# PSUM as three fixed groups of neighbouring banks, VectorE products over two banks at once, and a new order of the opening, in a fused sketch-attention and MLP kernel

## The chip, the cores and the metric

The kernel runs on one core of a Trainium2 chip. The metric is device time in microseconds (us), the median of several executions. A single execution can fall in a slower state (over 1.5% above the fastest run of the same kernel on the chip); such runs are listed but not compared. The engines are TensorE (PE in the profile, its weight loads PEld), VectorE (DVE), ScalarE (ACT), GpSimd (POOL) and the DMA queues issued by SyncE (SPq). PSUM is the memory that TensorE writes to. The program uses eight banks of it, each 128 partitions by 512 float32.

## The reference, cut to what matters

```python
# q, k, v: (4, 4, 1088, 32); S1, S2: (8, 32); w_in: (128, 2048), w_out: (2048, 128)
def phi(x):                              # sketch: 8 x 8 products of two projections
    a = einsum('rd,bhsd->bhsr', S1, x); b = einsum('rd,bhsd->bhsr', S2, x)
    return einsum('bhsi,bhsj->bhsij', a, b).reshape(..., 64)
q_p, k_p = phi(q), phi(k)
kv, z = einsum('bhsf,bhsd->bhfd', k_p, v), sum(k_p, axis=2)
x = (q_p @ kv) / (q_p @ z + 1e-6)        # attention without softmax
out = gelu_exact(x @ w_in) @ w_out       # 4352 tokens
```

The inputs are float64 words in memory; the kernel converts them on the way in (the class `Rounding`, seven small instructions for each piece on VectorE, ScalarE or GpSimd).

## The kernel before

The 4352 tokens go through the MLP as eight chunks of 512 columns and one of 256. For each chunk there are 16 *steps*: one hidden product with 128 rows of `w_in`, its Gelu, and the output product that belongs to the step two earlier (`LAG = 2`). The attention work of the following chunk is put into slots between these steps: turning the keys, their features, the expansion of the queries, the attention products ("attend").

Each of the eight banks is a tile of its own, handed out in turn by three pools:

```python
hps = ctx.enter_context(tc.tile_pool(name="hps", bufs=2, space=PSUM))
ops = ctx.enter_context(tc.tile_pool(name="ops", bufs=2, space=PSUM))
wps = ctx.enter_context(tc.tile_pool(name="wps", bufs=4, space=PSUM))

def work_bank():
    return wps.tile([128, CW], FP, name="w_ps")       # CW = 512
# ... hidden_bank and out_bank alike, from hps and ops

def hidden(n, fi):
    ps = hidden_bank()
    pe.matmul(ps[:, :W], lhsT=w_tile(w_in_sb, fi), rhs=xT[n][:, :W], start=True, stop=True)
    act.activation(out=g_of[n, fi][:, :W], in_=ps[:, :W], func=ACT.Gelu)
    # ...

def query_expand(n):
    expand_products(n)                # 4 matmuls into 4 work banks
    for g in range(4):
        expand_copy(n, g)             # ScalarE: half of the bank's rows to SBUF
        expand_multiply(n, g)         # VectorE: copy x other half, two 64x256 products

def key_features(b, r, banks, by_pool=()):
    # ... 16 matmuls of 32 columns into each of two banks, then for each bank
    for t in (1, 0):
        act.copy(out=a[:, t, :, 0:R], in_=ab[:, :, 0:R])
        dve.tensor_mul(**spread(k_p[b, r][:, t], a[:, t, :, 0:R], ab[:, :, R:2 * R]))

for t in range(len(steps) + LAG):
    # ...
    hidden(*steps[t])
    for f in slots[t]:                # attention work of the next chunk
        f()
    if t >= LAG:
        project(*steps[t - LAG])
```

## Time and profile before

| | before |
|---|---|
| time, median of the first three runs | 297.54 us (296.82 to 298.98) |
| span of the profiled execution | 297.3 us |
| TensorE busy | 285.6 us (96%) |
| VectorE, ScalarE busy | 124.2 us (42%), 135.4 us (46%) |
| first hidden product starts | 21.52 us |
| one full step (512 columns), one narrow step (256) | 1.72 us, 0.88 us |

How to read it: TensorE has almost no idle time after the first 32 us, so everything that other engines do counts only where it makes TensorE wait. The lines of these views stand in the prediction. One more view is used below: the list of start times of the 144 hidden products, from the timeline. The difference between two neighbours is what one step costs, with everything that lies in its slot.

### The profile page before, as it was taken

To read this page: it belongs to the slowest core of one execution; us is meant where nothing else is said; L and a number is where in the kernel's file an instruction comes from. 1 tells how busy PE (TensorE), PEld (TensorE's weight loads), DVE (VectorE), ACT (ScalarE), POOL (GpSimd) and SP (SyncE) were. 2 spreads that over 40 slices of the span, in tenths; PEclk is the share of its full clock that TensorE was granted. 3 is DMA by queue.
4 is the path that set the end of the run, shared out by engine and by line. 5 is a ranking of instruction groups with operands and counts; after the bars stand their busy time and mean duration, and the time that the engine had idled before them with its cause. 6 is when DMAs were issued, how large, how long until landed. Compare 5 with 4: busy or idle time off the path is not lost.

```text
span 297.3 us, 3821 instructions
## 1 busy us (share of the span) xinstructions
PE 285.6 (96%) x1497; PEld 139.3 (47%) x1497; DVE 124.2 (42%) x218; ACT 135.4 (46%) x261; POOL 17.4 (6%) x47
## 2 busy tenths in 40 slices
PE   6989899899999999999999999999999999999993
PEld 4653345453444444543443345543444344444693
DVE  5668468627441445423702374251713171322000
ACT  4476466327633562335534553256335633443341
POOL 2315120020000000020000000000000000000000
PEclk9599999999999999999999999999999999999998
DMA  6429759300002100020002000200002000200010
GB/s 212 159 70 366 203 147 255 67 0 0 0 9 34 31 0 0 2 38 0 1 0 35 1 2 0 36 2 0 0 0 38 0 0 0 35 2 0 12 23 20
DMA packets 32561, 13.37 MB, mean 45 GB/s; under 512 B 21408, under 2 KB 31904, under 8 KB 32544
## 3 DMA queue, kind: packets, MB, share of 16 engines
q1 hardware_dynamic: 32304, 13.05, 17.1%
q8 instruction: 12, 0.20, 0.3%
q10 hardware_dynamic: 240, 0.08, 0.1%
q14 instruction: 5, 0.04, 0.0%
HBM read 10.90 MB, written 2.23 MB: 44 GB/s over the span
## 4 chain that ended last, share of the span: by engine, by line
PE 91%; DVE 3%; ACT 2%; DMA 1%; issue 1%; POOL 0%; SPq 0%; ACTq 0%
PE h_ps L450 38%; PE o_ps L465 37%; PE w_ps L369 3%; PE o_ps L462 2%; PE w_ps L400 2%; PE w_ps L329 2%; DMA q<-in_q_dram 1%; PE w_ps L296 1%; PE o_ps L329 1%; PE w_ps L258 1%; DVE x_tok L431 1%; DVE q_pT L384 1%; ACT bits_r L214 1%; DVE bits_e L227 1%; PE h_ps L425 0%
## 5 line engine op out<-in xcount | busy, mean ns | idle before, releaser
L452 ACT ACTIVATE g<-h_ps 128x512 f32<-128x512 f32 (+1 forms) x144 | 82.4, 573 | 135.3 <-PE h_ps L450 135.0
L450 PE MATMUL h_ps<-xT,w_in 128*128 128x512 f32 (+1 forms) x288 | 140.3, 570 | 1.4 <-ACT xT L260 1.4
L465 PE MATMUL o_ps<-g,w_out 128*128 128x512 f32 x256 | 133.1, 602 | 0.4 <-POOL w_out L232 0.4
L450 PEld LDWEIGHTS h_ps<-xT,w_in 128*128 128x128 f32 x288 | 53.6, 190 | 63.8 <-issue 59.5
L465 PEld LDWEIGHTS o_ps<-g,w_out 128*128 128x128 f32 x256 | 46.3, 190 | 58.5 <-issue 56.8
L384 DVE TENSOR_TENSOR q_pT<-A_sb,w_ps 64x256 f32<-64x256 f32 (+1 forms) x72 | 29.4, 409 | 27.9 <-ACT A_sb L375 26.5
L407 DVE RECIPROCAL den<-den 128x512 f32<-128x512 f32 (+1 forms) x7 | 21.9, 3124 | 42.5 <-ACT den L406 42.5
L475 DVE STREAM_TRANSPOSE oT<-o_ps 128x512 f32<-128x512 f32 x8 | 5.7, 717 | 45.5 <-PE o_ps L465 45.5
L375 ACT COPY A_sb<-w_ps 64x512 f32<-64x512 f32 (+1 forms) x36 | 17.6, 557 | 4.1 <-PE w_ps L369 4.0
L411 DVE TENSOR_TENSOR xT<-w_ps,den 32x512 f32<-32x512 f32 (+1 forms) x28 | 18.2, 649 | 1.0
L406 ACT ACTIVATE den<-w_ps 32x512 f32<-32x512 f32 (+1 forms) x28 | 15.6, 557 | 2.9 <-PE w_ps L400 2.6
L271 POOL COPY v_aug<-v 128x512 f32<-128x512 f32 x8 | 5.3, 669 | 92.8 <-issue 62.0
L369 PE MATMUL w_ps<-qT,Srep 32*128 32x512 f32 x64 | 10.1, 702 | 0.0
L462 PEld LDWEIGHTS o_ps<-w_out,g 128*128 128x128 f32 x64 | 9.4, 191 | 0.7
L462 PE MATMUL o_ps<-w_out,g 128*128 128x128 f32 x64 | 9.4, 275 | 0.0
L310 DVE TENSOR_TENSOR k_p<-a_t,w_ps 128x512 f32<-128x512 f32 x12 | 7.4, 681 | 3.9 <-ACT a_t L309 3.9
L400 PE MATMUL w_ps<-q_pT,kz 64*64 64x512 f32 (+1 forms) x80 | 7.2, 459 | 0.0
L329 PEld LDWEIGHTS w_ps<-k_p,v_aug 128*64 128x64 f32 x192 | 5.8, 138 | 2.3 <-issue 2.3
L214 ACT ACTIVATE bits_r<-bits_e,below 128x512 uint32<-128x512 uint32 (+2 forms) x11 | 6.6, 610 | 0.6 <-DVE bits_e L206 0.6
L222 DVE SCALAR_TENSOR_TENSOR bits_m<-bits_a,bits_low 128x512 f32<-128x512 uint32 (+2 forms) x8 | 4.8, 605 | 4.8 <-ACT bits_low L202 4.3
L329 PE MATMUL w_ps<-k_p,v_aug 128*64 128x64 f32 x192 | 6.3, 224 | 0.0
L260 DVE COPY kT<-w_ps 128x512 f32<-128x512 f32 x6 | 3.9, 684 | 4.5 <-PE w_ps L258 4.5
(118 smaller groups left out, 117.8 us busy)
## 6 DMA issues: line engine op xcount, KB each, us to landing
v<-in_v_dram SPq DMA_DIRECT2D x4, 512.0 KB, 5.4
raw_w_in<-in_moe_w_in_dram SPq DMA_DIRECT2D x3, 512.0 KB, 4.5
raw_w_out<-in_moe_w_out_dram SPq DMA_DIRECT2D x3, 512.0 KB, 7.4
k<-in_k_dram SPq DMA_DIRECT2D x3, 512.0 KB, 5.0
q<-in_q_dram SPq DMA_DIRECT2D x24, 64.0 KB, 4.3
out_dram<-oT SPq DMA_DIRECT2D x24, 64.0 KB, 2.2
k<-in_k_dram SPq DMA_DIRECT2D x2, 256.0 KB, 2.9
q<-in_q_dram SPq DMA_DIRECT2D x2, 256.0 KB, 4.4
```

Of the source, the lines that this page charges most:

```text
L329: pe.matmul(ps[c * 64:(c + 1) * 64, r * F:(r + 1) * F], lhsT=v_aug[:, 2 * c + r, i, :], rhs=k_p[b, r][:, t, c * 4 + ch * 2 + one].rearrang ...
L369: pe.matmul(B_of[n][g][:, :W], lhsT=Srep[rows].rearrange("p a i j -> p (a i j)"), rhs=qT[n][rows].rearrange("p h j t -> p (h j t)"), start ...
L375: act.copy(out=A[g][F:, :width[n]], in_=B_of[n][g][:F, :width[n]])
L384: dve.tensor_mul(out=cols[r * F:(r + 1) * F, :, g], in0=a[:, r::2], in1=b[:, r::2])
L400: pe.matmul(banks[r][c * F:(c + 1) * F, c0:c1], lhsT=kz[b][r * F:(r + 1) * F, c, :], rhs=qp[n][r * F:(r + 1) * F, c, c0:c1], start=True, s ...
L406: act.activation(out=den[h * D:(h + 1) * D, :W], in_=banks[r][at:at + D, :W], func=ACT.Copy, bias=1e-6)
L407: dve.reciprocal(out=den[:, :W], in_=den[:, :W])
L411: dve.tensor_mul(out=xT[n][rows, :W], in0=banks[h % 2][rows, :W], in1=den[rows, :W])
L450: pe.matmul(ps[:, :W], lhsT=w_tile(w_in_sb, fi), rhs=xT[n][:, :W], start=True, stop=True)
L452: act.activation(out=g_of[n, fi][:, :W], in_=ps[:, :W], func=ACT.Gelu)
L462: pe.matmul(o_of[n][:, i * 128:(i + 1) * 128], lhsT=g[:, i * 128:(i + 1) * 128], rhs=w_tile(w_out_sb, fi), start=(first and i == 0), stop= ...
L465: pe.matmul(o_of[n], lhsT=w_tile(w_out_sb, fi), rhs=g, start=first, stop=final)
```

## The change

Its intent: with the banks of a group next to each other in one tile, one VectorE instruction can read two banks, so eight products of an expansion become four, and the attention by token needs one reciprocal and one product instead of two. In the opening, the sketches come before the first query turn and the pieces of the weight conversion are spread among waits; three later pieces also move one step earlier.

```diff
-    hps = ctx.enter_context(tc.tile_pool(name="hps", bufs=2, space=PSUM))
-    ops = ctx.enter_context(tc.tile_pool(name="ops", bufs=2, space=PSUM))
-    wps = ctx.enter_context(tc.tile_pool(name="wps", bufs=4, space=PSUM))
-    def work_bank():
-        return wps.tile([128, CW], FP, name="w_ps")
     ...
+    psum = ctx.enter_context(tc.tile_pool(name="psum", bufs=1, space=PSUM))
+    class Banks:
+        def __init__(self, name, n):
+            self.all, self.n, self.next = psum.tile([128, n, CW], FP, name=name), n, 0
+        def one(self):
+            self.next += 1
+            return self.all[:, (self.next - 1) % self.n]
+        def two(self):
+            self.next += self.next % 2 + 2
+            at = (self.next - 2) % self.n
+            return self.all[:, at:at + 2]
+    h_banks, o_banks, w_banks = Banks("h_ps", 2), Banks("o_ps", 2), Banks("w_ps", 4)
     ...
     def query_expand(n):
         expand_products(n)
         for g in range(4):
             expand_copy(n, g)
-            expand_multiply(n, g)
+            if g % 2:
+                expand_multiply(n, g // 2)      # two banks in one product
     ...
     key_turn(0, 0, hidden_bank(), by_act)
+    sketches()
     query_turn(0)
-    sketches()
     key_turn(0, 1, hidden_bank(), by_act)
     ... (then the expansion of chunk 0 interleaved with the key sums,
          and the parts of w_in[0], w_in[1], w_out[0] moved between them)
```

More of the change, by code (lines that the diff above doesn't have):

```diff
@@ L59 @@
     mlp = ctx.enter_context(tc.tile_pool(name="mlp", bufs=2))
-    hps = ctx.enter_context(tc.tile_pool(name="hps", bufs=2, space=PSUM))
-    ops = ctx.enter_context(tc.tile_pool(name="ops", bufs=2, space=PSUM))
-    wps = ctx.enter_context(tc.tile_pool(name="wps", bufs=4, space=PSUM))
-    def work_bank():
-        return wps.tile([128, CW], FP, name="w_ps")
-    def hidden_bank():
-        return hps.tile([128, CW], FP, name="h_ps")
-    def out_bank():
-        return ops.tile([128, CW], FP, name="o_ps")
+    psum = ctx.enter_context(tc.tile_pool(name="psum", bufs=1, space=PSUM))
[10 more added lines that the diff above has]
+    h_banks, o_banks, w_banks = Banks("h_ps", 2), Banks("o_ps", 2), Banks("w_ps", 4)
+    hidden_bank, out_bank, work_bank = h_banks.one, o_banks.one, w_banks.one
     by_act, by_dve, by_pool = act.copy, dve.tensor_copy, pool.tensor_copy
@@ L295, in key_features @@
                     at = i * 128 + c * 64
-                    pe.matmul(banks[t][c * 64:(c + 1) * 64, i * 32:(i + 1) * 32],
+                    pe.matmul(banks[c * 64:(c + 1) * 64, t, i * 32:(i + 1) * 32],
                               lhsT=kT[r][t * 64:(t + 1) * 64, at:at + 64],
@@ L303, in key_features @@
         for t in (1, 0):
-            ab = banks[t][:, :128].rearrange("p (n r) -> p n r", r=2 * R)
+            ab = banks[:, t, :128].rearrange("p (n r) -> p n r", r=2 * R)
             if t in by_pool:
@@ L365, in expand_products @@
         W = width[n]
-        B_of[n] = [work_bank() for g in range(4)]
+        B_of[n] = [w_banks.two() for g in range(2)]
         for g in range(4):
             rows = slice(g * D, (g + 1) * D)
-            pe.matmul(B_of[n][g][:, :W], lhsT=Srep[rows].rearrange("p a i j -> p (a i j)"),
+            pe.matmul(B_of[n][g // 2][:, g % 2, :W], lhsT=Srep[rows].rearrange("p a i j -> p (a i j)"),
                       rhs=qT[n][rows].rearrange("p h j t -> p (h j t)"), start=True, stop=True)
@@ L373, in expand_copy, with expand_multiply @@
     def expand_copy(n, g):
-        A[g] = att.tile([128, CW], FP, name="A_sb", bufs=4)
-        act.copy(out=A[g][F:, :width[n]], in_=B_of[n][g][:F, :width[n]])
-    def expand_multiply(n, g):
+        if g % 2 == 0:
+            A[g // 2] = att.tile([128, 2, CW], FP, name="A_sb", bufs=2)
+        act.copy(out=A[g // 2][F:, g % 2, :width[n]], in_=B_of[n][g // 2][:F, g % 2, :width[n]])
+    def expand_multiply(n, i):
         W = width[n]
-        a, b = (t[F:, :W].rearrange("f (h j t) -> f h j t", h=H, t=32) for t in (A[g], B_of[n][g]))
-        to = "f n (g j t) -> f n g j t" if n < NMAIN else "f n (j g t) -> f n g j t"
-        cols = qp[n][:, :, :W].rearrange(to, g=G, t=32)
-        for r in range(2):
-            dve.tensor_mul(out=cols[r * F:(r + 1) * F, :, g], in0=a[:, r::2], in1=b[:, r::2])
+        a, b = (t[F:, :, :W].rearrange("f g (h x) -> f g h x", h=H) for t in (A[i], B_of[n][i]))
+        if n < NMAIN:
+            cols = qp[n].rearrange("f n (g x) -> f g n x", g=G)[:, 2 * i:2 * i + 2]
+        else:
+            cols = qp[n][:, :, :W].rearrange("f n (j g t) -> f g n j t", g=G, t=32)[:, 2 * i:2 * i + 2]
+            a, b = (x.rearrange("f g h (j t) -> f g h j t", t=32) for x in (a, b))
+        for r in range(2):
+            if n < NMAIN:
+                dve.tensor_mul(out=cols[r * F:(r + 1) * F], in0=a[:, :, r::2], in1=b[:, :, r::2])
+            else:
+                for g in range(2):
+                    dve.tensor_mul(out=cols[r * F:(r + 1) * F, g], in0=a[:, g, r::2], in1=b[:, g, r::2])
     def query_expand(n):
@@ L413, with attend_by_token @@
     x_tok = {}
-    def attend_by_token(n, banks, between=lambda: None):
+    def attend_by_token(n, banks):
         x_tok[n] = att.tile([128, JC, H, D], FP, name="x_tok", bufs=1)
-        to = x_tok[n].rearrange("p j (c r) d -> p (j c) r d", r=2)
         den = att.tile([128, 2, JC * NP], FP, name="den_tok")
@@ L423, in attend_by_token @@
                     for r in range(2):
-                        rows, at, tok = slice(r * F, (r + 1) * F), (i * NP + c) * C, i * 128 + half * 64
-                        pe.matmul(banks[r][half * 64:(half + 1) * 64, at:at + C], lhsT=qp[n][rows, c, tok:tok + 64],
+                        rows, at, tok = slice(r * F, (r + 1) * F), (i * NP + c) * C + 1 - r, i * 128 + half * 64
+                        pe.matmul(banks[half * 64:(half + 1) * 64, r, at:at + C], lhsT=qp[n][rows, c, tok:tok + 64],
                                   rhs=kz[n // NCH][rows, c, (0, D - 1)[r]:(C, 2 * D)[r]], start=True, stop=True)
         for r in range(2):
-            nd = banks[r][:, :JC * NP * C].rearrange("p (g c) -> p g c", c=C)
+            nd = banks[:, r, 1 - r:1 - r + JC * NP * C].rearrange("p (g c) -> p g c", c=C)
             dve.tensor_scalar(out=den[:, r], in0=nd[:, :, (D, 0)[r]], scalar1=1e-6, scalar2=None, op0=AX.add)
-            dve.reciprocal(out=den[:, r], in_=den[:, r])
-            dve.tensor_mul(out=to[:, :, r], in0=nd[:, :, r:r + D],
-                           in1=den[:, r, :, None].broadcast_to([128, JC * NP, D]))
-            if r == 0:
-                between()
+        dve.reciprocal(out=den, in_=den)
+        nd = banks[:, :, 1:1 + JC * NP * C].rearrange("p r (g c) -> p r g c", c=C)
+        dve.tensor_mul(out=x_tok[n].rearrange("p j (c r) d -> p r (j c) d", r=2), in0=nd[:, :, :, 0:D],
+                       in1=den[:, :, :, None].broadcast_to([128, 2, JC * NP, D]))
     def turn_x(n, ps, copy):
@@ L501 @@
     key_turn(0, 0, hidden_bank(), by_act)
+    sketches()
     query_turn(0)
-    sketches()
     key_turn(0, 1, hidden_bank(), by_act)
     widen_v(0, 0)
-    banks = [out_bank(), out_bank()]
+    banks = o_banks.two()
     key_features(0, 0, banks)
-    key_features(0, 1, [hidden_bank(), hidden_bank()], by_pool=(1,))
+    key_features(0, 1, h_banks.two(), by_pool=(1,))
     widen_v(0, 1)
     widen_v_rem(0)
-    key_turn_rem(0, banks[1], by_act)
     expand_products(0)
+    w_in = [Rounding(w) for w in w_in_sb[:2]]
+    w_in[0].fields()
     expand_copy(0, 0)
+    key_turn_rem(0, banks[:, 1], by_act)
+    expand_copy(0, 1)
     expand_multiply(0, 0)
-    key_features_rem(0, banks[1])
     kv_bank = out_bank()
     kv_sum(0, kv_bank, 0)
-    for g in range(1, 4):
-        expand_copy(0, g)
+    expand_copy(0, 2)
+    key_features_rem(0, banks[:, 1])
+    expand_copy(0, 3)
+    expand_multiply(0, 1)
     kv_sum(0, kv_bank, 1)
     kv_sum_rem(0, kv_bank)
-    for g in range(1, 4):
-        expand_multiply(0, g)
+    w_in[0].exponents()
     take_kv(0, kv_bank, by_act)
@@ L528 @@
     by_act(**late[0])
-    r = Rounding(w_in_sb[0])
-    r.fields()
-    r.exponents()
-    r.low_words()
+    w_in[0].signs()
+    w_in[1].fields()
+    w_in[0].low_words()
+    w_in[0].mantissas(by_pool=True)
+    load_rest()
+    w_in[0].product(pool)
+    w_in[1].low_words()
+    w_in[1].exponents()
     keep_busy(1, hidden_bank())
-    attend_by_token(0, [hidden_bank(), hidden_bank()], r.signs)
+    attend_by_token(0, h_banks.two())
     expand_products(1)
-    r.mantissas(by_pool=True)
-    load_rest()
-    r.product(pool)
-    r = [Rounding(w) for w in (w_in_sb[1], w_out_sb[0])]
-    for x in r:
-        x.low_words()
     keep_busy(1, out_bank())
+    w_out = [Rounding(w) for w in w_out_sb[:2]]
+    w_out[0].low_words()
     for g in range(2):
         expand_copy(1, g)
-    for x in r:
-        x.fields()
+    w_in[1].mantissas()
+    w_in[1].signs()
+    w_in[1].product(pool)
+    w_out[0].fields()
     turn_x(0, hidden_bank(), by_act)
-    r[0].mantissas()
-    for x in r:
-        x.exponents()
-    for x in r:
-        x.signs()
-    r[0].product(pool)
-    r[1].mantissas(by_pool=True)
-    r[1].product(pool)
-    w_out_next = Rounding(w_out_sb[1])
-    w_out_next.fields()
+    w_out[0].exponents()
+    expand_multiply(1, 0)
+    w_out[0].mantissas()
+    w_out[0].signs()
+    w_out[0].product(pool)
+    w_out[1].fields()
     steps = [(n, fi) for f in range(0, NF, 4) for n in range(2) for fi in range(f, f + 4)]
@@ L570, in features @@
     def features(b, r):
-        key_features(b, r, [work_bank(), work_bank()])
+        key_features(b, r, w_banks.two())
     held = {}
@@ L592, in round_at @@
         at(t + 1, lambda: (r[0].exponents(), r[0].finish()))
-    at(0, expand_multiply, 1, 0)
-    at(0, lambda: (w_out_next.low_words(), w_out_next.exponents(), w_out_next.signs()))
-    at(1, lambda: (w_out_next.mantissas(by_pool=True), w_out_next.product(pool)))
-    for g, t in ((1, 0), (2, 1), (3, 1)):
-        if g > 1:
-            at(t, expand_copy, 1, g)
-        at(t, expand_multiply, 1, g)
-    at(3, lambda: attend_by_token(1, [work_bank(), work_bank()]))
-    for i, (t0, t1) in enumerate(((4, 6), (9, 11), (13, 20))):
+    at(0, lambda: (w_out[1].low_words(), w_out[1].exponents()))
+    for g in range(2, 4):
+        at(1, expand_copy, 1, g)
+    at(1, expand_multiply, 1, 1)
+    at(1, lambda: (w_out[1].mantissas(), w_out[1].signs(), w_out[1].product(pool)))
+    at(3, lambda: attend_by_token(1, w_banks.two()))
+    for i, (t0, t1) in enumerate(((4, 6), (8, 10), (12, 20))):
         round_at(t0, w_in_sb[i + 2])
```

## The prediction

> **What bounds the kernel now.** I read the page first (busy shares, slices, chain that ended last), then the timeline of the opening and of one step of the steady part, then the groups of instructions.
>
> ```profile
> PE 285.6 (96%) x1497; PEld 139.3 (47%) x1497; DVE 124.2 (42%) x218; ACT 135.4 (46%) x261; POOL 17.4 (6%) x47
> PEclk9599999999999999999999999999999999999998
> PE 91%; DVE 3%; ACT 2%; DMA 1%; issue 1%; POOL 0%; SPq 0%; ACTq 0%
> ```
>
> TensorE is busy for 96% of the span and is 91% of the chain. VectorE and ScalarE are below half, so saved VectorE work is worth nothing unless TensorE waits for it. TensorE waits only in the opening (before about 32 us) and in the tail. The clock row shows one dip: the finer windows put half clock from 8.1 to 14.9 us.
>
> The steady part is 144 steps (128 of 512 columns, the last 16 of 256). A step is one hidden product (L450), its Gelu on ScalarE (L452), and the output product (L465) of two steps earlier. One step:
>
> ```profile
> 84.71 0.19 PEld L450 LDWEIGHTS h_ps<-xT,w_in 128*128 128x128 f32 x1 [0.24 <-issue]
> 85.14 1.02 PE L450 MATMUL h_ps<-xT,w_in 128*128 128x512 f32 x2
> 86.00 1.02 PE L465 MATMUL o_ps<-g,w_out 128*128 128x512 f32 x2
> 86.20 0.60 ACT L452 ACTIVATE g<-h_ps 128x512 f32<-128x512 f32 x1 [1.12 <-PE h_ps L450]
> 86.43 0.19 PEld L450 LDWEIGHTS h_ps<-xT,w_in 128*128 128x128 f32 x1 [0.24 <-issue]
> 86.86 1.02 PE L450 MATMUL h_ps<-xT,w_in 128*128 128x512 f32 x2
> ```
>
> The hidden product ends at 85.14 + 1.02 = 86.16, its Gelu runs 86.20 to 86.80, and the next hidden product starts at 86.86, a period of 1.72 us with TensorE full. But that product's weight load was already issued at 86.43, 0.37 us before the Gelu ended. The overlap exists only because the next product does not wait for this Gelu. How a product starts that does wait:
>
> ```profile
> 31.29 0.58 ACT L260 COPY xT<-w_ps 128x512 f32<-128x512 f32 x1 [3.65 <-PE w_ps L258]
> 31.93 0.30 PEld L450 LDWEIGHTS h_ps<-xT,w_in 128*128 128x128 f32 x2 [0.91 <-ACT xT L260]
> 31.93 1.13 PE L450 MATMUL h_ps<-xT,w_in 128*128 128x512 f32 x2 [0.68 <-ACT xT L260]
> ```
>
> The copy ends at 31.87; weight load and product start 0.06 us later (0.05 to 0.15 elsewhere in the opening), and the product takes 1.13 instead of 1.02, since its first weight load is no longer hidden.
>
> **What the Trainium skill says.** "PSUM — Partial Sum Buffer", Specifications (TRN2), says ScalarE and VectorE use PSUM in parallel at full bandwidth as long as they do not meet in a bank; nothing there asks engines in different banks to wait. The trace agrees: the Gelu above reads one hidden bank while TensorE fills others. "VectorE: DVE Perf Modes", Side-by-side, has a fixed cost of some 150 cycles per instruction; here 256 elements take 0.43 us back to back (two 64x256 products in 0.86) and 512 take 0.68, so about 0.17 us is fixed. "TensorE: Matmul & The Clock Gate", Part 1, says that the clock is halved after a poorly used window of 3.413 us; the dip here lasts 6.83 us, two such windows. The same page, Architectural detail, says TensorE pulls weight loads ahead of running matmuls: seen above, and seen not to happen where the product waits.
>
> **The change, part by part.** I built both programs and resolved each wait to the instruction that releases it. That decides this case. Before, each PSUM bank is a tile of its own. After, the 2 + 2 + 4 banks are three tiles, and in the built program a wait covers the whole tile, not the bank. Of 144 hidden products 139 wait for a Gelu; before, all 139 wait for the Gelu of two steps earlier (their own bank), after, all 139 for that of the step just before (the other bank). Reads of different banks by ScalarE and VectorE are ordered too: the third expand copy waits for the VectorE products of the first pair.
>
> *Hidden to Gelu to hidden, full steps.* Hidden ends at 0; Gelu 0.04 to 0.64; +0.06; product 1.13: the period is 0.04 + 0.60 + 0.06 + 1.13 = 1.83 against 1.72, so +0.11. Steps with other TensorE work behind the hidden product (about 27) hide it. About 100 steps x 0.11 = +11.
>
> *Narrow steps.* Before, 0.88 each (product starts at 287.34, 288.21). The Gelu of 288.85 ends at 289.23, yet the next weight load started at 288.98; it would now start at 289.29, 0.31 later. 16 x 0.31 = +5.
>
> *Query expansion.*
>
> ```profile
> L384 DVE TENSOR_TENSOR q_pT<-A_sb,w_ps 64x256 f32<-64x256 f32 (+1 forms) x72 | 29.4, 409 | 27.9 <-ACT A_sb L375 26.5
> L310 DVE TENSOR_TENSOR k_p<-a_t,w_ps 128x512 f32<-128x512 f32 x12 | 7.4, 681 | 3.9 <-ACT a_t L309 3.9
> L375 ACT COPY A_sb<-w_ps 64x512 f32<-64x512 f32 (+1 forms) x36 | 17.6, 557 | 4.1 <-PE w_ps L369 4.0
> ```
>
> Eight products of 0.43 become four of about 0.70 (from L310's size): 0.6 us of VectorE saved per chunk, off the path. But copies and products now take turns: products of TensorE end at 1.07 after the hidden product, two copies (0.53 each) to 2.18, two VectorE products to 3.63, two copies 3.68 to 4.74, only then the next Gelu to 5.34, and the hidden product behind it ends at 5.34 + 0.06 + 1.13 = 6.53, against 1.07 + 2 x 1.83 = 4.73. +1.8 for each of six full chunks, +0.5 for the narrow one: +11.
>
> *Attend.* Four denominators of 0.58 start when all of its matmuls are done (1.07) and end at 3.37; Gelu to 3.97, hidden ends at 5.16 against 1.02 + 3.66 = 4.68: +0.5 x 6 = +3.
>
> *Keys, three batches.* The second turn waits for VectorE's copy of the first (0.68 + latencies): 0.85. The second group of feature matmuls waits for copy, product, copy, product of the first group, in turn: 0.25 + 0.70 + 0.25 + 0.70 + 0.06 = 1.96. Together 2.8 x 3 = +8.
>
> *Stores.* The first output product of a chunk now waits for the transpose of the other bank (0.72), but a hidden product (0.86) lies between: 0.
>
> *Opening.* Sketches before the transpose take S off the wait for q (the masked sketch at 5.6 instead of 6.83). The token attend loses a reciprocal, a product and the signs from between (2.0 to about 1.2 us). Conversion pieces move up, so the waits for w_in (0.7) and w_out (1.2) go. Against this the same whole-tile waits: rem features wait for the first expand pair, the second batch of kv sums for the rem product, the q turn for the kv copy. Worked through in order, the first hidden product starts at about 20.7 instead of 21.5, and chunk 1 at about 31.4 instead of 31.9: about -1.
>
> *Clock.* Expansion leaves TensorE idle for about 1.75 us, features for 1.96. The windows of 3.4 us that hold such a gap are 43 to 50% busy. In the trace the one at 4.7 to 8.1 (about 58% busy with small matmuls) was followed by half clock, the one at 28.6 to 32.0 (also 58%) was not. A dip costs about 3 us. Nine gaps; I take two dips, +6, and this is the part I know least.
>
> Sum: 11 + 5 + 11 + 3 + 8 - 1 + 6 = +43, so 297.5 + 43 = 341 us.
>
> **Rivals.** (1) The opening's gain stands and the waits cost nothing: 295 to 296. For it: TensorE has a Gelu's slack in the order of work (0.86 us of output product against 0.64). Against it: that slack is measured to the product's start; the weight load waits too, and ScalarE's other work stands before the next Gelu. (2) Only the opening and the keys suffer because the weight load is after all not held: the 1.83 falls to 1.72 and the sum to about 325. Against it: the load at 31.93 waited with its product. (3) The clock falls at most gaps: 9 x 3 = 27 instead of 6, about 360.
>
> **Range and chances.** The known terms give 335; latencies of 0.10 instead of 0.06 add 5, no dips and a freer load take off 10, many dips add 20. I take 341, 8 in 10 between 325 and 359. Slower by over 2% means over 303.5, which the expansions, keys and narrow steps (24 us) reach alone: 0.95. Within 2%: 0.03, faster: 0.02, mostly for my having misread what the waits do.
>
> **What would show it.** Right: in the steady part the Gelu group's start to start is about 1.83 us and the hidden weight load is released by ScalarE right after a Gelu; the expand copies show idle time ended by VectorE's q_pT; TensorE's busy share falls to about 85 to 88%; feature matmuls wait about 2 us for k_p; the first Gelu comes about 0.8 us earlier. Wrong: a steady period of 1.72 (the load is not held), or half clock over many slices (the stalls are dearer than their length).

## The result, and the profile after

| | before | after |
|---|---|---|
| time, median | 298.15 us (4 runs, 296.82 to 298.98) | 343.36 us (4 runs, 340.6 to 352.64; the 352.64 is slow) |
| ratio of the fast runs | | 1.149 (95% interval 1.140 to 1.158) |
| span of the profiled execution | 297.3 us | 341.2 us |
| first hidden product starts | 21.52 us | 25.85 us |

A ratio here is the mean time of one kernel's fast runs over that of the other's fast runs of the same rounds, so it is not quite the ratio of the medians.

The page of the changed kernel (busy time by engine, granted clock in 40 slices, chain that ended last):

```profile
PE 309.0 (91%) x1497; PEld 135.8 (40%) x1497; DVE 120.9 (35%) x184; ACT 136.4 (40%) x259; POOL 15.6 (5%) x45
PEclk9999999999999999999999999699999999999999
PE 75%; ACT 14%; DVE 9%; issue 2%; DVEq 0%
```

VectorE has 34 instructions fewer and is 3.3 us less busy: the part of the change that was intended works. But ScalarE and VectorE, 5% of the chain before, are now 23% of it. TensorE's busy time went up by 23 us although it executes the same 1497 products; part of that is half clock, part is products whose first weight load is no longer hidden (1.12 instead of 1.02 us for a pair, next view).

A plain step of the steady part, in the timeline (start, duration, engine and line, operation, in brackets the idle time before it and what ended it):

```profile
94.46 0.30 PEld L466 LDWEIGHTS h_ps<-xT,w_in 128*128 128x128 f32 x2 [0.66 <-ACT g L468]
94.47 1.12 PE L466 MATMUL h_ps<-xT,w_in 128*128 128x512 f32 x2
95.43 1.02 PE L481 MATMUL o_ps<-g,w_out 128*128 128x512 f32 x2
95.63 0.60 ACT L468 ACTIVATE g<-h_ps 128x512 f32<-128x512 f32 x1 [1.22 <-PE h_ps L466]
96.28 0.30 PEld L466 LDWEIGHTS h_ps<-xT,w_in 128*128 128x128 f32 x2 [0.66 <-ACT g L468]
```

The Gelu ends at 95.63 + 0.60 = 96.23, and the weight load of the next hidden product starts 0.05 us later, released by it. Before, that load ran while the Gelu was still busy. The period is 96.28 - 94.46 = 1.82 us (1.81 on average).

An expansion of the steady part:

```profile
107.21 1.12 PE L466 MATMUL h_ps<-xT,w_in 128*128 128x512 f32 x2
...
109.47 1.06 ACT L383 COPY A_sb<-w_ps 64x512 f32<-64x512 f32 x2 [0.50 <-PE w_ps L376]
...
110.56 1.40 DVE L397 TENSOR_TENSOR q_pT<-A_sb,w_ps 64x512 f32<-64x512 f32 x2 [5.34 <-ACT A_sb L383]
...
111.99 1.06 ACT L383 COPY A_sb<-w_ps 64x512 f32<-64x512 f32 x2 [1.46 <-DVE q_pT L397]
113.07 0.60 ACT L468 ACTIVATE g<-h_ps 128x512 f32<-128x512 f32 x1
...
113.72 1.13 PE L466 MATMUL h_ps<-xT,w_in 128*128 128x512 f32 x2 [1.54 <-ACT g L468]
```

Read down: two copies, two products, two copies, in turn. ScalarE idles 1.46 us for VectorE although the second pair of copies reads other banks than the products do. The Gelu stands behind the copies in ScalarE's queue, and TensorE idles 1.54 us for the Gelu. Over the whole span, the view of waits adds up as follows (us in total, times, longest):

```profile
PEld h_ps L466 <- ACT g L468: 84.5, 117, 2.4
...
ACT A_sb L383 <- DVE q_pT L397: 10.2, 7, 1.5
```

The first line is idle time of the weight loads, most of it beside running products, so it isn't the loss. What matters is that it is there at all, 117 times.

The keys of one batch:

```profile
132.22 0.66 PE L265 MATMUL w_ps<-ident,k 128*128 128x128 f32 x4 [0.79 <-DVE kT L267]
...
134.52 0.67 PE L303 MATMUL w_ps<-S,kT 64*64 64x32 f32 x32
137.21 0.67 PE L303 MATMUL w_ps<-S,kT 64*64 64x32 f32 x32 [2.02 <-DVE k_p L317]
```

The second key turn waits for the copy of the first, and the second group of feature products for all the work on the first group.

The opening:

```profile
8.56 2.09 PE L376 MATMUL w_ps<-qT,Srep 32*128 32x512 f32 x8
...
21.88 2.09 PE L376 MATMUL w_ps<-qT,Srep 32*128 32x512 f32 x8
...
25.85 1.10 PE L466 MATMUL h_ps<-xT,w_in 128*128 128x512 f32 x2 [0.81 <-ACT xT L267]
```

The eight expand products take 1.14 us at full clock (so they do in the steady part). Here they take 2.09, at 8.56 and still at 21.88: TensorE was at half clock through the opening. The page's clock row doesn't show it. The trace's first clock record is the rise at 23.9 us, and the row prints nines where it has no record. In the kernel before, the clock was full from 4.7 to 8.1 us, half to 14.9, and full from there.

From the list of hidden products, the 43.9 us between the two spans divide so (before, after, and the difference, in the profiled executions):

| where | predicted | measured | how |
|---|---|---|---|
| plain full steps | +11 | +9.1 | 82 steps that are 0.10 longer (8.0 in sum), and five pairs at stores, 0.22 a pair |
| narrow steps | +5 | +4.2 | 1.17 instead of 0.88, the first 1.52 |
| expansions | +11 | +10.8 | 1.78 + 5 x 1.71, and 0.47 in the narrow chunk |
| attend | +3 | +3.1 | 6 x 0.52 |
| keys, three batches | +8 | +9.6 | 3.0, 3.3, and 3.3 without the dip behind it |
| clock dip in the steady part | +6 | +3.0 | one, of 6.83 us, behind the third key batch |
| opening, to the first hidden product | -1 | +4.3 | 25.85 against 21.52; chunk 1 follows by the same +4.3 |
| sum | +43 | +44.1 | the tail behind the last hidden product is 0.4 shorter |

### The profile page after: what moved, and what is told of

It is laid out like the page before. It is cut to its first block, busy times and chain, and to the rows that moved or that the text cites. A ratio compares the mean times of both kernels' runs of the same rounds, so it can differ in the third digit from the quotient of the medians.

```text
span 341.2 us, 3780 instructions
## 1 busy us (share of the span) xinstructions
PE 309.0 (91%) x1497; PEld 135.8 (40%) x1497; DVE 120.9 (35%) x184; ACT 136.4 (40%) x259; POOL 15.6 (5%) x45
## 4 chain that ended last, share of the span: by engine, by line
PE 75%; ACT 14%; DVE 9%; issue 2%; DVEq 0%
PE h_ps L466 33%; PE o_ps L481 24%; ACT A_sb L383 4%; ACT den L423 4%; PE w_ps L376 3%; ACT g L468 3%; DVE q_pT L397 2%; PE o_ps L478 2%; PE w_ps L417 2%; PE w_ps L336 2%; DVE k_p L317 2%; PE w_ps L303 1%; PE o_ps L336 1%; PE w_ps L265 1%; PE w_ps L509 1%
## 5 line engine op out<-in xcount | busy, mean ns | idle before, releaser
L466 PE MATMUL h_ps<-xT,w_in 128*128 128x512 f32 (+1 forms) x288 | 151.8, 609 | 15.1 <-ACT g L468 13.3
L481 PE MATMUL o_ps<-g,w_out 128*128 128x512 f32 x256 | 135.3, 611 | 0.0
L466 PEld LDWEIGHTS h_ps<-xT,w_in 128*128 128x128 f32 x288 | 45.8, 190 | 100.4 <-ACT g L468 84.5
L481 PEld LDWEIGHTS o_ps<-g,w_out 128*128 128x128 f32 x256 | 46.4, 192 | 59.2 <-issue 55.2
L397 DVE TENSOR_TENSOR q_pT<-A_sb,w_ps 64x512 f32<-64x512 f32 x32 | 22.1, 691 | 35.1 <-ACT A_sb L383 34.9
L383 ACT COPY A_sb<-w_ps 64x512 f32<-64x512 f32 (+1 forms) x36 | 18.4, 553 | 17.5 <-DVE q_pT L397 10.2
L317 DVE TENSOR_TENSOR k_p<-a_t,w_ps 128x512 f32<-128x512 f32 x12 | 8.2, 687 | 10.9 <-ACT a_t L316 10.9
L376 PE MATMUL w_ps<-qT,Srep 32*128 32x512 f32 x64 | 11.0, 764 | 0.0
L303 PE MATMUL w_ps<-S,kT 64*64 64x32 f32 x192 | 4.4, 234 | 6.1 <-DVE k_p L317 6.1
L229 DVE SCALAR_TENSOR_TENSOR bits_m<-bits_a,bits_low 128x512 f32<-128x512 uint32 (+2 forms) x10 | 6.1, 608 | 3.7 <-ACT bits_low L209 3.1
L303 PEld LDWEIGHTS w_ps<-S,kT 64*64 64x64 f32 x192 | 3.7, 148 | 8.7 <-DVE k_p L317 6.4
```

Source lines behind the costliest of these rows:

```text
L376: pe.matmul(B_of[n][g // 2][:, g % 2, :W], lhsT=Srep[rows].rearrange("p a i j -> p (a i j)"), rhs=qT[n][rows].rearrange("p h j t -> p (h j ...
L383: act.copy(out=A[g // 2][F:, g % 2, :width[n]], in_=B_of[n][g // 2][:F, g % 2, :width[n]])
L397: dve.tensor_mul(out=cols[r * F:(r + 1) * F], in0=a[:, :, r::2], in1=b[:, :, r::2])
L481: pe.matmul(o_of[n], lhsT=w_tile(w_out_sb, fi), rhs=g, start=first, stop=final)
```

## The experiments

All were compared with the kernel before on the same chip. A *group* below means banks that share a tile. Medians of all runs, and ratios of fast runs to fast runs of before:

| label | what it is | time, us | ratio (95%) |
|---|---|---|---|
| h_alone | changed kernel, only the two hidden banks apart | 312.66 | 1.052 (1.043 to 1.060) |
| pairs | hidden and output banks apart, work banks as two pairs | 296.44 | 0.996 (0.989 to 1.002) |
| singles | all banks apart, one-bank products, new order | 294.49 | 0.989 (0.983 to 0.995) |
| grouped | kernel before with three groups, nothing else | 365.94 | 1.219 (1.209 to 1.230) |
| after_again | changed kernel, unchanged | 342.72 | 1.142 (1.136 to 1.148) |
| copies_first | four copies before the products in expansions | 331.38 | 1.108 (1.102 to 1.114) |
| features_together | both feature groups before copies and products | 340.27 | 1.134 (1.127 to 1.140) |
| warm | one idle product in the opening | 341.75 | 1.141 (1.137 to 1.144) |
| hidden_pair | as singles, but the two hidden banks share a tile | 314.54 | 1.052 (1.047 to 1.057) |
| pairs_apart | as pairs, the key turns from different tiles | 294.42 | 0.985 (0.981 to 0.989) |
| singles_again | singles once more, more rounds | 295.04 | 0.988 (0.984 to 0.993) |

The median of before was 298.84 us beside the first four, 299.26 beside the next four and 299.13 beside the last three. All results were correct.

### The hidden banks apart

```diff
-    h_banks, o_banks, w_banks = Banks("h_ps", 2), Banks("o_ps", 2), Banks("w_ps", 4)
+    # Banks(name, banks, banks in one tile)
+    h_banks, o_banks, w_banks = Banks("h_ps", 2, 1), Banks("o_ps", 2, 2), Banks("w_ps", 4, 4)
```

> The changed kernel with one edit: the two hidden banks are two tiles again, the output and work banks stay grouped. In the built program 133 hidden products wait for the Gelu of two steps earlier, as before the change. Theory (whole-tile waits): the steady step falls from 1.81 to 1.72 us, the narrow one from 1.19 to 0.88, and a late Gelu behind expand copies or denominators costs almost nothing; of the 45 us lost some 28 come back (11 + 5 + 9 of 11 + 3): about 315 us, 309 to 320. Rival (the loss lies in the new order of the opening, in clock dips and in the two-bank products): hidden waits are a small part, 335 us or more.

It measured 312.66 us, inside the expected range: 30.7 of the 45 us are gone. The same expansion as above:

```profile
102.09 1.06 ACT L398 COPY A_sb<-w_ps 64x512 f32<-64x512 f32 x2 [0.50 <-PE w_ps L391]
...
104.61 1.06 ACT L398 COPY A_sb<-w_ps 64x512 f32<-64x512 f32 x2 [1.46 <-DVE q_pT L420]
104.63 1.02 PE L494 MATMUL h_ps<-xT,w_in 128*128 128x512 f32 x2
```

Copies and products still take turns, with the same 1.46 us. But the second hidden product starts at 104.63, 4.70 us after the one at 99.93, exactly as in the kernel before. Taking turns in the work group costs TensorE nothing here, because TensorE doesn't wait for the Gelu behind the copies. What remains over the run with all banks apart (16.5 us by span) lies, step by step, in the keys (11.8 us, with a dip of 3.4 us in the first batch) and in the opening (3.1 us); the steps, the expansions and the attends add about 2 us. Of these, 1.1 lie at five stores (5 x 0.22): there the first output product of a chunk waits for the transpose of the other output bank, which still shares its tile.

### The hidden banks together, all others apart

```diff
+    h_banks, o_banks, w_banks = Banks("h_ps", 2, 2), Banks("o_ps", 2, 1), Banks("w_ps", 4, 1)
     (one-bank products, as in singles)
```

> The counterpart to the run with the hidden banks apart: here only the two hidden banks share a tile, all other banks are tiles of their own, one-bank products, new order in the opening. Theory (the losses add only where two waits meet): 82 plain steps x 0.10 = 8, narrow steps 4, six attends x 0.5 = 3, five stores x 0.22 = 1, but next to nothing at the six expansions (at most 0.2 each), because the expand copies no longer take turns with the products and so do not hold up the Gelu: 294.5 + 17 = 311 to 313. Rival: the expansions lose their 1.7 us to the wait for the Gelu alone: 294.5 + 27 = 321 or more.

It measured 314.54 us. The span is 19.3 us above that of singles, and the list of hidden products divides it: 1.9 at the first hidden product, 0.9 in the rest of the opening, 9.9 in steps that differ by at most 0.12, 3.7 in the narrow steps, 6 x 0.50 = 3.0 in the attends, at most 0.24 in any expansion. In its expansion the four copies of ScalarE run without a break:

```profile
98.67 2.02 ACT L398 COPY A_sb<-w_ps 64x512 f32<-64x512 f32 x4 [0.45 <-PE w_ps L391]
...
100.72 0.60 ACT L496 ACTIVATE g<-h_ps 128x512 f32<-128x512 f32 x1
101.36 0.30 PEld L494 LDWEIGHTS h_ps<-xT,w_in 128*128 128x128 f32 x2 [0.77 <-ACT g L496]
```

So the theory holds: the 1.7 us of an expansion need both groups at once, the hidden group (TensorE waits for the Gelu just before) and the work group (that Gelu stands behind copies which wait for products). Either group alone leaves the expansion as it was. It is 1.5 us above the expected range. The 1.9 us at the first hidden product are clock: it came up at 13.6 us here and at 4.6 in singles, and a second execution of singles, with the clock up at 13.8, starts its first hidden product at 20.12, here 20.13. (The on-record text counts five stores at 0.22. Those belong to the output group, which is apart here: the steps at stores are 0.10 longer, like the plain ones. In the changed kernel one of them reads "PEld L481 LDWEIGHTS o_ps<-g,w_out" at 179.24, after 0.68 us idle ended by the transpose oT. Since the next step then loses nothing, a store costs 0.22 where two plain steps cost 0.20, so next to nothing on top.)

### Smaller tiles, and none at all

```diff
-    h_banks, o_banks, w_banks = Banks("h_ps", 2), Banks("o_ps", 2), Banks("w_ps", 4)
+    h_banks, o_banks, w_banks = Banks("h_ps", 2, 1), Banks("o_ps", 2, 1), Banks("w_ps", 4, 2)   # pairs
+    h_banks, o_banks, w_banks = Banks("h_ps", 2, 1), Banks("o_ps", 2, 1), Banks("w_ps", 4, 1)   # singles
```

> The changed kernel with every bank a tile of its own where one bank is used at a time (hidden, output), and the work banks as two tiles of two banks; two-bank products of the expansion stay, so does the whole new order. Theory: nearly all is back, only the second key turn waits for the first copy twice (about 0.9 us each) and the third expand copy waits for nothing of the other pair: 297 to 301 us. Rival 1 (the new order or the two-bank products themselves cost): 305 or more. Rival 2 (the new order is worth a us or two, as intended): 295 to 297.

> The changed kernel with all eight banks as tiles of their own and products over one bank at a time: only the new order of the opening is left of the change. Theory: no wait on another bank is left, 296 to 299 us, i.e. the same as before within 2%, with the first hidden product about as early as before or up to 1 us earlier if the clock of the opening is the same. Rival (the order of the opening alone costs the 4.3 us by which the first hidden product is late in the changed kernel): 301 to 303.

Both came out just below their ranges, at 296.44 (which is what rival 2 of that text named) and 294.49 us. In singles the banks come from fixed tiles that are handed out by hand, as in the changed kernel, so giving up the pools is not what costs. The new order is a gain by itself: in singles the first hidden product starts at 18.26 us instead of 21.52 (20.12 in the execution of singles with the late clock, so up to 1.9 us of this is clock), 0.96 us come at one step of the first key batch, where TensorE of the kernel before waited 0.76 us for VectorE's copy of the keys, and nothing is lost later. Pairs loses 1.00 us against singles in each of two key batches and nowhere else. There the second key turn takes the other bank of the same tile and waits for the first one's copy.

### The grouping alone

```diff
-    hps / ops / wps pools, one tile for each bank
+    h_banks, o_banks, w_banks = Banks("h_ps", 2), Banks("o_ps", 2), Banks("w_ps", 4)
     (everything else as before: one-bank products, old order)
```

> The kernel before with one edit: its eight banks are taken from three tiles (2 + 2 + 4), nothing else; order and one-bank products are those of before. In the built program all 139 hidden waits are on the Gelu one step earlier, and copies and products of the expansion take turns bank by bank. Theory: this alone makes the loss, and the expansion, in four turns instead of two, costs more than in the changed kernel (about 1.4 us more in each of six chunks): 340 to 352 us. Rival (the two-bank products or the order carry the loss): 300 to 315.

It measured 365.94 us; two of the four runs are slow, the fast ones are 362.91 and 363.37. That is 64 us above before, and 11 above the top of the expected range. Its profile fell in the slow state, so only its pattern is read, not its total:

```profile
PEclk9998599799899989999899999998999899999998
...
129.24 1.40 PE L451 MATMUL h_ps<-xT,w_in 128*128 128x512 f32 x2 [3.06 <-ACT g L453]
```

The clock row has dips in seven places before the tail (slices 3 and 4 are one; slice 7 holds two, so eight dips). In the changed kernel the slow profile (after_again) has three in the steady part and the fast one has one, so part of this may be the state. But the fast runs say the same more mildly: their recorded mean clock is 0.955 and 0.969 here, 0.975 to 0.994 in the changed kernel. The expansion now goes in four turns of copy and products instead of two, TensorE idles 3.06 us for the Gelu, and the two hidden products are 8.02 us apart (121.22 to 129.24), 6.51 in the changed kernel, 4.70 before. So within the grouped program the two-bank products are worth 1.5 us an expansion, and probably fewer clock dips. Each full expansion of the steady part is 3.22 us longer than in the kernel before, about as expected (1.8 + 1.4), so what went over the range lies elsewhere; how it divides between opening and dips is not settled, for want of a fast profile. With the new order they take back some 20 us (363 against 342). Product form and order together repair part of a damage that the grouping does.

### Parts undone inside the grouped program

```diff
     # copies_first, in query_expand
         for g in range(4):
             expand_copy(n, g)
-            if g % 2:
-                expand_multiply(n, g // 2)
+        for i in range(2):
+            expand_multiply(n, i)
     # features_together, in the slots of a key batch
-        for r in range(2):
-            at(t - 17, features, b, r)
+        at(t - 17, features_both, b)     # both groups of matmuls, four copies, four products
```

> One part undone: in the six full expansions of the steady part the four copies of ScalarE stand before the four products of VectorE, so that they no longer take turns; the tiles stay grouped. Theory: hidden product to second hidden product across an expansion falls from 6.52 to 1.07 + 4 x 0.53 + 0.06 + 0.60 + 0.06 + 1.13 = about 5.0 us, 1.5 us each, so 9 us less than the changed kernel of the same rounds, about 334, and perhaps 3 us more if a clock dip goes with it. Rival: the loss of an expansion comes from the two-bank products themselves holding the tile until they end: then Gelu still waits for them, 6.5 stays, and the time stays within 2 us of the changed kernel.

> One part undone: in the three key batches of the steady part both groups of feature matmuls are issued before any copy, then the four copies, then the four products; the tiles stay grouped. Theory: the wait of 1.96 to 2.02 us of the second group for the products of the first disappears, 3 x 2 = 6 us less than the changed kernel, about 337.5, and the clock dip seen behind one such wait may go too (3 us more). Rival: the wait only moves to a later one (the Gelu behind four copies, or the kv sums behind the products): less than 2 us gained.

copies_first measured 331.38 us against 342.72 for the changed kernel of the same rounds, a gain of 11.3 (expected 9). In its expansion:

```profile
107.30 2.02 ACT L383 COPY A_sb<-w_ps 64x512 f32<-64x512 f32 x4 [0.50 <-PE w_ps L376]
...
109.35 0.60 ACT L468 ACTIVATE g<-h_ps 128x512 f32<-128x512 f32 x1
...
110.00 0.30 PEld L466 LDWEIGHTS h_ps<-xT,w_in 128*128 128x128 f32 x2 [0.82 <-ACT g L468]
```

Each of the six full expansions became 1.55 us shorter in the list, which is 9.3, and the narrow one 0.47; the rival (the products themselves hold the tile against the Gelu) falls. The rest of the difference between the two profiles is clock: the one dip of this one lasts 3.4 us instead of 6.8, and the opening, with the clock up at 19.5 instead of 23.9, was 2 us shorter.

features_together measured 340.27 us, only 2.4 less by median. By the total alone the rival (under 2) would nearly have won. The list says otherwise: at each key batch the wait for the features is gone, 2.22 us each (not counting the dip behind the third). In the first batch 1.20 us of it come back a step later, where the turn of the remainder keys now waits for the four products, so it is 5.5 us in all. What hid it is the opening of this execution. Its first clock record is a rise at 38.0 us, and it lost 0.9 us up to the first hidden product and 4.6 more up to the first of chunk 1, against the changed kernel's profile. Three of its four runs took 340.2 to 340.4 us and one 337.07.

### The clock of the opening

> The changed kernel once more, unchanged, to see whether its slow opening is its own or luck. My theory: most of the 4.3 us that the opening lost comes from TensorE at half clock until 23.8 us, which the run before the grouping's other parts show is not a must (with the hidden banks apart the clock was full from about 6 us, and the first hidden product came at 21.37). If that is luck of one execution, this profile may show full clock early and the first hidden product at 21 to 23 us; the time would then be 339 to 341. Rival: the opening's own gaps hold the clock down every time: half clock beyond 15 us again, first hidden product at 25 to 26.5, time 342 to 345.

> The changed kernel with one idle product added in the opening, behind the sketch transpose, where TensorE waited 0.38 us for the copy of the first key turn; it fills that gap and delays the second key turn by at most 0.6 us. Theory: the opening loses because the clock stays at half; with TensorE busy without a gap from 1.2 to about 10 us the full clock comes by about 8 us, the first hidden product at about 22, and the time is some 3 us less than the changed kernel, 340. Rival: whole-tile waits make the opening long, whatever the clock: first hidden product at 25 to 26.5, time as the changed kernel or 0.5 us more.

```diff
     # warm
     sketches()
+    keep_busy(1, out_bank())       # one product of zeros
     query_turn(0)
```

Two lines of the changed kernel run again:

```profile
7.26 1.14 PE L376 MATMUL w_ps<-qT,Srep 32*128 32x512 f32 x8
...
18.82 2.09 PE L376 MATMUL w_ps<-qT,Srep 32*128 32x512 f32 x8
```

The very same instructions at 7.26 us took 1.14 this time instead of 2.09. The clock was full from 4.2 to 14.4 us, then half to 34.9. Here is the opening in all executions that were profiled. The first four kernels have the same opening program, warm has one product more, and "grouped" has the old order:

| profiled execution | TensorE at full clock | first hidden product | first of chunk 1 |
|---|---|---|---|
| after | from 23.9 | 25.85 | 36.22 |
| after_again (slow) | 4.2 to 14.4, then from 34.9 | 23.68 | 38.59 |
| copies_first | from 19.5 | 23.88 | 34.25 |
| features_together | from 38.0 | 26.73 | 41.66 |
| warm | 6.8 to 13.7, then from 20.5 | 23.66 | 34.03 |
| grouped (slow) | 20.7 to 34.4, then from 44.6 | 25.89 | 40.46 |
| h_alone | 6.1 to 12.9, then from 16.4 | 21.37 | 31.45 |
| singles | from 4.6 | 18.26 | 28.20 |
| singles_again | from 13.8 | 20.12 | 30.07 |
| hidden_pair | from 13.6 | 20.13 | 30.95 |
| pairs | from 4.5 | 18.14 | 27.78 |
| pairs_apart | from 5.5 | 18.01 | 27.66 |
| before | 4.7 to 8.1, then from 14.9 | 21.52 | 31.93 |

The two rows of singles are one program in two executions: a rise 9.2 us later costs 1.9 us at the first hidden product. In the six profiles with all three groups the clock was full for the rest of the opening only from 19.5 us or later; in the six with output banks apart from 14.9 at the latest (h_alone, with output banks together: 16.4). So neither text of after_again is quite right. The slow opening is not the same each time, as my theory had it, but it was never fast either, as the rival had it. In warm the clock did come up at 6.8 us, and was lost again at 13.7, where TensorE sat idle for 1.79 us:

```profile
14.00 1.97 PE L336 MATMUL o_ps<-k_p,v_aug 128*64 128x64 f32 x32 [1.79 <-DVE k_p_rem L329]
```

That wait is one of the whole-tile waits: the second set of key sums writes an output bank whose neighbour in the group is still read by the product for the remainder keys. The other two executions with grouped output banks whose clock had come up early lost it near the same wait: after_again (2.11 us of idle up to 13.10, clock lost at 14.43) and h_alone (1.79 us up to 13.11, lost at 12.94). In singles and pairs, where only a later product waits for the same VectorE instruction (1.29 us up to 12.56, 0.95 us up to 12.46), the clock stayed. That ties the lost clock to the waits, but no experiment removed this wait alone, so it is not shown as the cause. Warm's first hidden product, at 23.66, lies between its two texts (about 22, and 25 to 26.5). Its time, 341.75 against 342.72 us (fast runs 340.56 to 341.78 against 339.75 to 343.22), shows no gain; as a cure it failed.

### A version that beats both

```diff
     # pairs_apart, on top of pairs
     def turn_keys(b, r):
+        w_banks.next += r          # the second turn from the other pair of banks
         key_turn(b, r, work_bank(), by_dve)
```

> The work banks as two tiles of two banks each with the two-bank products, hidden and output banks each their own tile, as in the run called pairs, but the two key turns of a batch come from different tiles, so that the second need not wait for the copy of the first. Theory: the 1.0 us that pairs lost to singles at each of two key batches goes: about 294.5, level with singles within 0.5 us, and 1.1% to 1.4% below the kernel before; a two-bank product is then worth nothing by itself, as its time lay beside TensorE's work. Rival: the wider products make the expansions or the opening shorter for TensorE as well: 293 or less.

> The kernel with every bank a tile of its own, one-bank products and only the new order of the opening, once more beside pairs_apart, as a candidate to beat both kernels: 294.5, 1.1% below the kernel before, with the first hidden product at about 18.3 us against 21.5. Rival: its lead was a matter of that chip or of the clock in the opening: within 0.5% of before.

pairs_apart measured 294.42 us (294.13 to 294.7), 1.5% below the kernel before, singles_again 295.04, 1.2% below; both intervals exclude 1. After the opening the two lists of hidden products agree to 0.05 us in sum (apart from -0.35 at one step of the opening). So the two-bank products, though VectorE is busy for 120.8 us instead of 125.9 in singles, give TensorE nothing from the first chunks on; what both kernels gain over before is the new order. Whether pairs_apart is really better than singles these runs don't decide: their profiled openings differ in clock (full from 5.5 against 13.8 us).

## Why the prediction was right or wrong

**The total was right** (341 predicted, 343.36 measured, range 325 to 359), and so was the mechanism behind most of it. "In the built program a wait covers the whole tile, not the bank" is shown from both sides: taking the groups apart takes the loss away (singles, pairs), making them in the old kernel makes it (grouped), and each group has its own share (h_alone, hidden_pair).

**Hidden to Gelu to hidden.** Predicted period 1.83, measured 1.81, since the release took 0.05 instead of 0.06 us and the product 1.12 instead of 1.13. The rival that the load "is after all not held" falls: 117 loads of hidden products are released by a Gelu. The count of such steps was taken as 100 and is about 92.

**Narrow steps.** The step was put 0.31 us later and measured 0.29.

**Query expansion and attend.** Predicted 6.53 us from hidden end to hidden end; the trace has 113.72 + 1.13 - 108.33 = 6.52. Attend was predicted 5.16 and is 5.26 (122.61 + 1.12 - 118.47), mostly as four denominators take 2.38 instead of 2.32 us (and the prediction's 3.37 should be 1.07 + 4 x 0.58 = 3.39). What the prediction did not say, and the experiments show, is that the expansion's loss is a product of two groups: it vanishes when either is taken apart.

**Stores.** Predicted 0. The wait for the other bank's transpose is there (five times), and alone it costs 0.22 (h_alone), but beside the hidden waits it adds next to nothing.

**Keys.** Predicted 2.8 a batch, measured 3.0 to 3.3: 1.0 for the turn (0.85 predicted) and 2.2 for the features (1.96). The idle times themselves are 0.79 and 2.02. The rest, some 0.2 us at each wait, fits a product that starts with its weight load exposed, which the prediction had counted for hidden products only; no run tested this.

**Opening: this is the step that failed.** "Worked through in order, the first hidden product starts at about 20.7 instead of 21.5 [...] about -1" was wrong by 5 us. The order of work in it was fine. It took the durations of the opening from the trace of before, with that execution's clock: half up to 4.7 us and for two windows of 3.4 us from 8.1, the rest full. In the changed kernel the clock was at half up to 23.9 us, so each product before that took up to twice as long. The Trainium skill, "TensorE: Matmul & The Clock Gate", Part 1, says the 3.4 us windows run free of the kernel's start, so that the same kernel shows a different number of slow products from run to run. These runs agree that it differs (a rise at 4.6 and at 13.8 us for one program), and they show a size that the prediction lacked: 1.9 us in that program, and 23.7 to 26.7 us for the first hidden product of the changed opening. How much of the loss is clock and how much the whole-tile waits as such can only be estimated, since no execution had all the groups and an undisturbed clock. On full clock (up to 14.4; only this part of the slow execution is used) after_again reached its query turn, the transposes of q, at 14.84 us; singles, on full clock too, at 12.94. So up to there the waits cost 1.9 us. From there to the first hidden product singles needs 5.3 us (18.26 - 12.94); with the hidden banks together it is 5.3 as well (hidden_pair, 14.83 to 20.13). Together 14.84 + 5.3 = 20.1, close to the predicted 20.7, which had these waits in it. By that estimate, of the 7.6 us between singles (18.26) and the changed kernel (25.85) about 2 are waits and the remaining 5 to 6 the clock. They are not independent, since the clock was lost near one of these waits (see warm). Two signs of being right failed with it: the first Gelu was to come 0.8 us earlier, and TensorE's busy share, forecast at 85 to 88% (290 to 300 us of 341), was 91% (309.0 us).

**Clock.** +6 was meant for two dips; the profiled execution had one of 6.83 us, which cost 3.0. It stands behind the 2.02 us of idle time in the third key batch; the same idle time in the second batch was followed by none. (In these traces the recorded clock changes lie whole multiples of 3.41 us apart, here 55 and 2 of them.) Adding the opening, the clock took by estimate 8 to 9 us against an undisturbed one. The term and the opening's were wrong in opposite directions and by 3 and 5 us, which is part of why the total came out so close.

**Rivals.** The first (the waits cost nothing, 295 to 296) names by chance what the new order gives once the groups are gone: 294.4 to 296.4. The third (a dip at most gaps) describes the grouping with one-bank products, which had eight dips in its (slow) profile.

## What to carry to other kernels

Before merging buffers so that one instruction can cover several, ask what the program will then wait for: if waits follow tiles, neighbours that were independent become ordered, and what it costs is decided by the engine that bounds the kernel (here TensorE, 45 us), not by the engine that the wider instruction relieves (VectorE, 3 us, none of it on the path). Make a merged tile as small as the widest instruction needs, and give work that must overlap different tiles: two-bank pairs taken in turn kept the wide products and lost nothing. When a total contradicts a theory, compare the two kernels step by step before dropping it: a gain of 5.5 us was there in features_together while its total showed 2.4, because the clock of the opening had taken the rest.

## What the Trainium skill lacked or had wrong

- "PSUM — Partial Sum Buffer" says that engines in different banks do not disturb each other, and to guard PSUM by bank. It doesn't say that a program whose banks share a tile can wait by the tile, though the banks differ; that took this kernel from 298 to 363 us (the grouping alone).
- "TensorE: Matmul & The Clock Gate", Architectural detail, has weight loads pulled ahead of running matmuls, but no case of a load that has to wait together with its product: here a pair of 512-column products then takes 1.12 instead of 1.02 us, 0.10 us in every plain step.
- The same page, Part 1, has full clock after one busy window and calls the ramp under 1% of a typical span. Here a window that was wholly busy by the profile (6.8 to 10.2 us in the changed kernel, mostly small products) did not bring it, and the rise came between 4.2 and 38.0 us in different executions. A delay of 9.2 us cost 1.9 us (0.6% of the span) in one program, and the changed kernel's half clock up to 23.9 us by estimate 5 to 6 us (over 1.5%). In the steady part one idle gap of 2.02 us was followed by 6.83 us at half clock, another of the same length by none. The page gives no busy share that raises or keeps the clock.
- The same page warns that clock events in a trace can be unreliable. More exactly, here there is no record before the first change: features_together printed a mean granted clock of 1.0 and nines throughout, while its expand products at 21.88 us took 2.09 instead of 1.14 us.
